# The sums of a feature DFT's result, moved from GpSimd to VectorE in single steps

## The chip, the cores and the metric

The kernel runs on one core of a Trainium2 chip. The metric is the device time of one execution in microseconds. The core has five engines that run side by side and meet through semaphores: TensorE (PE in the profile, its weight loads PEld) for matrix products, VectorE (DVE), ScalarE (ACT), GpSimd (POOL), and SyncE (SP), which here issues every DMA.

## The reference

The reference is a transformer block of two sublayers over 2048 tokens with 448 features. The first is Fourier mixing, the second a gated GELU network with 1792 hidden columns:

```python
def _A_ref(x, dft_seq_re, dft_seq_im, dft_hid_re, dft_hid_im):
    a = jnp.einsum("bsd,ed->bse", x, dft_hid_re)
    b = jnp.einsum("bsd,ed->bse", x, dft_hid_im)
    y = jnp.einsum("ts,bse->bte", dft_seq_re, a) - jnp.einsum("ts,bse->bte", dft_seq_im, b)
    return y

def _B_ref(x, w_gate, w_up, w_down):
    g = jnp.einsum("bsd,df->bsf", x, w_gate)
    u = jnp.einsum("bsd,df->bsf", x, w_up)
    h = _gelu(g) * u
    return jnp.einsum("bsf,fd->bsd", h, w_down)

h = x + _A_ref(_layernorm(x, axis=-1), A_dft_seq_re, A_dft_seq_im, A_dft_hid_re, A_dft_hid_im)
h2 = h + _B_ref(_layernorm(h, axis=-1), B_w_gate, B_w_up, B_w_down)
```

## The kernel before

All products are made from float16 operands split into a high and a low part (`hi_part` on ScalarE, `lo_part` on VectorE, lines 104 to 111), with three of the four cross terms kept.

The first half of the execution does the Fourier mixing. The tokens form 16 tiles of 128, in pairs ("units" 0 to 7). For each tile the **feature DFT** (`feature_mm`, slots "F") multiplies the normalized, transposed tile with the hidden DFT matrix into two PSUM banks `ab`, one real and one imaginary. The **sequence DFT** (`seq_mm`, slots "U") runs in 8 passes over the output tokens; in each pass every unit contributes once, with its weights `wr` loaded from HBM, split into `ws` on ScalarE and VectorE, and freed for the next load. In four of the units (`S_UNITS`: 4 to 7, tiles 8 to 15) the products go by Strassen's scheme with 7 instead of 8 block products. These need sums of the weights (`seq_sums` into `wsum`, VectorE, split into `wss`) and, once per tile, sums of the feature DFT's result: `feature_sums`. The order of units in the first pass is 0, 1, 5, 2, 6, 3, 7, 4, so that tiles 10 and 11 are the first that need `feature_sums`, then 12, 13, 14, 15, 8, 9.

For such a tile the chain is: `feature_high` (ScalarE copies the two banks to the float32 tile `b32`), `feature_sums` (three dependent operations on `b32`, lines 493 to 495, on GpSimd), `sums_high` (ScalarE, float16), `sums_low` (VectorE). For the other tiles `feature_high` (ScalarE) and `feature_low` (VectorE, line 111) read PSUM directly. Four PSUM banks serve the feature DFT, two per tile, so a tile's products can begin only when the tile before the last has been read out; the tiles come in the order ..., 10, 11, 4, 5, 12, 13, 6, 7, ....

Beside this, VectorE and ScalarE prepare the gated network's weights for 12 of 14 blocks (class `Weights`: `gu_raw` is loaded, `sums` makes `gu_s` on lines 639 to 645, four pieces are split into `gu_p` and stored to `w_dram`), and handle the finished passes (`seq_out`, moments, normalization, `ffn_sums`, splits and transposes).

The order on each engine is written by a **planner**. `add` makes a task with an engine, a cost, a due time and what it must follow; `chain` makes one task for each `yield` of a generator. `arranged` steps through time by 0.05 us; whenever an engine is free in its model, the ready task with the earliest due time begins. Due times follow `T`, the planned start of each slot of TensorE; planner time 0 is the start of slot 3, tile 3's feature DFT, at 24.05 us in the trace. The instructions are then issued in the order found, and each engine works through its queue strictly in this order. In the model a VectorE task that begins while GpSimd is busy counts 1.6 times. `feature_sums` is one GpSimd task of 3.4 us; the only other planned GpSimd task is `down_sums(0)` near the end of the DFTs. The weight blocks' due times are spread evenly from `begin0` to 10 us before the end of the DFTs; the first sums of a block may begin 10 us before its own start time.

The second half runs the gated network and the down projection; TensorE there is fed by `gw` loads from `w_dram`, and GpSimd does other sums.

Of the kernel before, what the change touches and what calls it, by code (L numbers as in the profile page):

```python
# [32 lines left out]
def kernel(  # L33
# [38 lines left out]
    V, A, G, PE = nc.vector, nc.scalar, nc.gpsimd, nc.tensor  # L72
# [257 lines left out]
    def x_load(u, parts=(slice(0, 2),)):  # L330
        if parts[0].start == 0:
            t = pair_tile(f"x{u}")
            for g in range(2):
                xt[2 * u + g] = t[:, g, :], t[:, parts[0], :]
        for s in parts:
            src = x_pairs[u][:, s, :]
            t = xt[2 * u + s.start]
            nc.sync.dma_start(t[1] if s.start == 0 else t[0], src if s.start == 0 else src[:, 0, :])
# [9 lines left out]
    def x_stats(*tiles):  # L348
        n, tag = len(tiles), f"x{tiles[0]}"
        mv = norm_x[tiles] = small.tile([P, n, 2], F32, tag=f"mv{n}", name=f"mv_{tag}")  # L350
        sts = [small.tile([P, 6], F32, tag="st", name=f"st_x{i}") for i in tiles]
        for i, st in zip(tiles, sts):
            V.bn_stats(st, xt[i][0])  # L353
        for g, st in enumerate(sts):
            V.bn_aggr(mv[:, g, :], st)

    def x_root(*tiles):
        norm_x[tiles] = norm_x[tiles], root(norm_x[tiles], f"x{tiles[0]}")

    def x_rstd_steps(*tiles):  # L360
        mv, sd = norm_x.pop(tiles)
        found = []
        steps = rstd_steps(found, mv, sd, f"x{tiles[0]}")
        next(steps)
        for g, i in enumerate(tiles):
            norm_x[i] = mv, found[0], g
        yield
        yield from steps

    def x_rstd(*tiles):  # L370
        for _ in x_rstd_steps(*tiles):
            pass

    def x_bias(*tiles):
        mv, r, _ = norm_x[tiles[0]]
        nb = small.tile([P, len(tiles)], F32, tag=f"nb{len(tiles)}", name=f"nb_x{tiles[0]}")
        bias_of(nb, mv, r)
        for i in tiles:
            norm_x[i] += (nb,)

    def x_norm(i):
        x_norm_v(i)
        x_high(i)
# [25 lines left out]
    def x_turn(i):  # L409
        xT_tile(i)  # L410
        nc.sync.dma_start_transpose(xT[i], xs[i])
# [79 lines left out]
    def feature_sums(i, E):  # L491
        b = b32[i]
        E.tensor_sub(b[:, 4:6], b[:, 0:1].to_broadcast([P, 2, HD]), b[:, 1:3])
        E.tensor_sub(b[:, 6], b[:, 2], b[:, 4])
        E.tensor_sub(b[:, 7], b[:, 3], b[:, 6])

    def sums_high(i):
        t = bop[i] = dft.tile([P, 2, 7, HD], F16, name=f"b{i}")
        hi_part(t[:, 0], b32[i][:, 1:8])
# [233 lines left out]
    FIRST = 3  # L733
    COST = {"F": 4.16, "P": 4.54, "S": 4.02}
    spans = [COST["F" if s[0] == "F" else "S" if is_s(s[2]) else "P"] for s in slots]
    T = {n: sum(spans[FIRST:n]) - sum(spans[n:FIRST]) for n in range(len(slots) + 1)}
    tasks, steps = [], {}

    def add(*args, **kw):
        tasks.append(Task(*args, **kw))  # L740
        return tasks[-1]

    def chain(engine, costs, due, make, after=()):

        run, last = [], list(after)

        def step(first):
            if first:
                run.append(make())
            next(run[0])  # L750

        for k, cost in enumerate(costs):
            last = [add(engine, cost, due, lambda k=k: step(k == 0), after=last)]
        return last[0]
# [4 lines left out]
    def fixed(n, rank, engine, cost, what, after=(), lag=0.0):  # L759
        if n < FIRST:  # L760
            plan(n, rank, what)
            return None
        return add(engine, cost, T[n + 1], what, after=after, begin=T[n] - 1.0, lag=lag)
# [3 lines left out]
    for k, (i, i2) in enumerate(tiles_of):  # L767
        n = where["F", i]
        if k > 2:
            t = fixed(n - 10, 8, "SP", 0.1, lambda u=i // 2: x_load(u), lag=5.0)  # L770
            t = fixed(n - 7, 7, "V", 1.35, lambda i=i, j=i2: x_stats(i, j), [t])
            t = fixed(n - 6, 2, "A", 0.3, lambda i=i, j=i2: x_root(i, j), [t])
            if n - 6 < FIRST:
                fixed(n - 6, 5, "V", 0.6, lambda i=i, j=i2: x_rstd(i, j))
            else:
                t = chain("V", (0.2, 0.1, 0.1, 0.1), T[n - 5], lambda i=i, j=i2: x_rstd_steps(i, j), [t])
            t = fixed(n - 6, 5, "V", 0.15, lambda i=i, j=i2: x_bias(i, j), [t])
        for c in (i, i2):
            n = where["F", c]
            if k > 2:  # L780
                low = fixed(n - 5, 5, "A", 1.15, lambda i=c: x_norm(i), [t])
                low = fixed(n - 5, 5, "V", 0.85, lambda i=c: x_lo(i), [low])
            if k >= 2:
                turned[c] = fixed(n - 4, 2, "SP", 0.1, lambda i=c: x_turn(i), [low] if k > 2 else (), lag=5.0)
                steps[n].after += [t for t in [turned[c]] if t]
        for c in (i, i2):
            n = where["F", c]
            if not k:
                continue
            done = [steps[n]] if n in steps else []  # L790
            if is_s(c // 2):
                t = drained = add("A", 1.05, T[n + 1] + 1.5, lambda i=c: feature_high(i), after=done + ring_w[-2:][:1] * (len(ring_w) > 1))
                t = add("G", 3.4, T[n + 2], lambda i=c: feature_sums(i, G), after=[t])
                t = add("A", 1.45, T[n + 2] + 2.0, lambda i=c: sums_high(i), after=[t])
                t = add("V", 1.7, T[n + 2] + 3.5, lambda i=c: sums_low(i), after=[t])
                ring_w.append(t)
            else:
                t = add("A", 0.95, T[n + 1] + 1.0, lambda i=c: feature_high(i), after=done)
                t = drained = add("V", 1.07, T[n + 1] + 2.5, lambda i=c: feature_low(i), after=[t])
            bop_of[c] = t  # L800
            out_of[n] = drained
# [11 lines left out]
    for g, (p, u) in enumerate(units):  # L813
        n = where["U", p, u]
# [14 lines left out]
        if is_s(u):  # L829
            t = chain("V", (0.6, 0.34, 0.34), T[n] - 3.0, lambda p=p, u=u: seq_sums(p, u), [load] + sums_of)  # L830
# [11 lines left out]
    for p in range(N_PASS):  # L842
        q, j = divmod(p, 2)
        of_pass = [where["U", p, u] for u in range(N_UNIT)]
        n0, n = min(of_pass), max(of_pass) + 1
# [12 lines left out]
        t = add("A", 0.25, t0 + 14.0, lambda q=q, j=j: ffn_root(q, j), after=m)  # L858
        t = chain("V", (0.2, 0.1, 0.1, 0.1), t0 + 15.0, lambda q=q, j=j: ffn_rstd_steps(q, j), [t])
        last_e, h_done[p] = m, [store, t]  # L860
        if q < 2:
            t = add("V", 0.15, t0 + 16.0, lambda q=q, j=j: ffn_bias(q, j), after=[t])
            t = add("A", 1.35, t0 + 17.0, lambda q=q, j=j: ffn_norm_act(q, j, hp[q, j]), after=[t])
            h_done[p] = [store, t]
            for k in range(4):
                t = add("V", 0.36, t0 + 18.0 + k, lambda q=q, j=j, k=k: ffn_sums(q, j, (k,)), after=[t])
            for k in range(2):
                high = add("A", (0.65, 1.0)[k], t0 + 22.0 + k, lambda q=q, j=j, k=k: ffn_hi(q, j, (k,)), after=[t])
                t = high
            for k in range(5):  # L870
                t = add("V", (0.34, 0.87, 0.25, 0.35, 0.25)[k], t0 + 23.0 + k, lambda q=q, j=j, k=k: ffn_lo(q, j, (k,)), after=[t])
# [17 lines left out]
        gu[f] = Weights(f, p2, None)  # L889

    plan(0, 9, lambda: gu_begin(order[0]))
    begin0 = 20.0
    raw, freed, stages = None, [], []
    for k, f in enumerate(order):
        gap = (at_end - 10.0 - begin0) / N_DFT
# [4 lines left out]
        t, lows = s2, []  # L900
        for m in range(4):
# [4 lines left out]
            t = high  # L906
# [7 lines left out]
    t = fixed(len(slots) - 14, 9, "SP", 0.1, lambda: down_load(0), last_e, lag=6.0)  # L914
# [2 lines left out]

    def arranged():

        now, left, busy, begun, n = 0.0, list(tasks), {"V": 5.6, "A": 4.7, "G": 0.0, "N": 0.0}, [], FIRST  # L920
        busy["SP"] = busy["PE"] = 0.0

        def ready(t):
            return t.begin <= now and all(a.end is not None and a.end + a.lag <= now for a in t.after)

        while left or n < len(slots):
            if n < len(slots) and busy["PE"] <= now and ready(steps[n]):
                steps[n].end = busy["PE"] = now + spans[n]
                begun.append((now, n))
                n += 1  # L930
            for engine in ("SP", "N", "V", "A", "G"):
                if busy[engine] > now:
                    continue
                able = [t for t in left if t.engine == engine and ready(t)]
                if able:
                    t = min(able, key=lambda t: t.due)
                    cost = t.cost * (1.6 if engine == "V" and busy["G"] > now else 1.0)
                    t.end = busy[engine] = now + cost
                    begun.append((now, t))
                    left.remove(t)  # L940
            now += 0.05
            assert now < 2 * at_end
        return begun
# [448 lines left out]
    for t in range(3 * NF, N_GU):  # L1392
        f = t % NF
        if f < NF - 1:
            n, k = divmod(f, 2)
# [196 lines left out]
```

## Time and profile before

| | us |
|---|---|
| Median of three runs | 718.97 |
| Lowest and highest | 717.75, 719.52 |
| The profiled execution | 719.33 |
| Its span, first to last instruction | 717.6 |
| TensorE busy in it | 707.3 |
| VectorE, ScalarE, GpSimd busy | 519.6, 396.4, 212.2 |

A timeline row gives the start in us, the time covered in us, engine, line, operation, what is written from what, the tile's form and a count; in square brackets stands the engine's idle time before it and what ended it. A row of waits reads: who waited for whom, us in total, times, the longest. A row of groups gives busy us and mean ns of one, then the idle time before. DVE line 111 and ACT line 105 are helpers, so such a row is told apart by its tile's name.

### The profile page before, as it was taken

Reading aid. Unit: us, or ns where it says so; the run is one execution under the profiler, and the core shown is the slowest. Engines: PE = TensorE matmul, PEld = TensorE weight load, DVE = VectorE, ACT = ScalarE, POOL = GpSimd, SP = SyncE. Lnnn points to the kernel's source line nnn. Section 1 sums busy time; section 2 is a strip of 40 time slices with the busy share of each in tenths; the row PEclk is TensorE's granted clock in tenths of the full one; section 3 lists DMA queues with packets and bytes.
Section 4 is the critical chain, followed back from the end, with each engine's and each line's share of the span. In section 5 each row is a group of like instructions: output and inputs, shape, how many; then the busy total and the mean of one; then the engine's idle time right before and its main releaser. Section 6 shows DMA issues by size and latency. Waiting matters only on the chain.

```text
span 717.6 us, 15058 instructions
## 1 busy us (share of the span) xinstructions
PE 707.3 (99%) x5944; PEld 575.6 (80%) x5944; DVE 519.6 (72%) x1054; ACT 396.4 (55%) x836; POOL 212.2 (30%) x241
## 2 busy tenths in 40 slices
PE   8998999999999999999999999999999999999998
PEld 5555567777776777686888899999999999999998
DVE  6898889999896988978368667575765756677520
ACT  5676655767474764645166575555555545555500
POOL 0033042000000000001015664375664755557230
PEclk9999999999999999999999999999999999999999
DMA  9466555887987898748258754847568686655401
GB/s 330 113 148 164 99 192 180 296 203 264 246 256 193 260 282 278 252 163 320 99 203 327 259 182 161 189 162 202 178 188 193 184 214 209 214 179 206 156 14 65
DMA packets 83815, 143.85 MB, mean 200 GB/s; under 512 B 41888, under 2 KB 60448, under 8 KB 83744
## 3 DMA queue, kind: packets, MB, share of 16 engines
q1 hardware_dynamic: 83744, 142.89, 64.8%
q8 instruction: 46, 0.75, 0.4%
q14 instruction: 25, 0.20, 0.1%
HBM read 113.38 MB, written 20.19 MB: 186 GB/s over the span
## 4 chain that ended last, share of the span: by engine, by line
PE 82%; DVE 10%; ACT 3%; DMA 2%; issue 2%; SPq 1%; DVEq 0%; ACTq 0%
PE acc L570 31%; PE pY L1173 13%; PE acc_d L1118 11%; PE pZ L1173 9%; PE pX L1173 9%; PE ab L456 5%; DMA wr<-in_w_seq_dram 1%; DVE ws L111 1%; PE last_Z L1335 1%; PE last_X L1335 1%; PE last_Y L1335 1%; DVE xs L109 1%; DMA wh_raw<-in_w_hid_dram 1%; DVE b L111 1%; DVE st_x L353 1%
## 5 line engine op out<-in xcount | busy, mean ns | idle before, releaser
L1173 PEld LDWEIGHTS <-gw 128*128 128x128 f16 x2184 | 213.4, 98 | 23.3 <-issue 1.4
L570 PE MATMUL acc<-b,ws 128*128 128x448 f16 (+1 forms) x1344 | 222.0, 312 | 0.1
L570 PEld LDWEIGHTS <-ws 128*128 128x128 f16 x1344 | 130.6, 98 | 71.1 <-DVE ws L111 0.4
L1173 PE MATMUL pY<-hops,gw 128*128 128x256 f16 x952 | 129.1, 273 | 0.0
L1118 PE MATMUL acc_d<-wd,dn_w 128*128 128x224 f16 x882 | 105.1, 259 | 0.0
L570 PE MATMUL acc<-b,wss 128*128 128x224 f16 x768 | 94.8, 259 | 0.7 <-DVE wss L111 0.7
L1118 PEld LDWEIGHTS <-dn_w 128*128 128x128 f16 x882 | 85.1, 98 | 2.8
L1173 PE MATMUL pZ<-hops,gw 128*128 128x256 f16 x616 | 85.5, 273 | 0.7 <-DVE hh L1183 0.6
L105 ACT ACTIVATE ws<-wr 128x256 f16<-128x256 f32 (+2 forms) x96 | 62.6, 690 | 40.8 <-DMA wr<-in_w_seq_dram 22.9
L1173 PE MATMUL pX<-hops,gw 128*128 128x256 f16 x616 | 83.3, 273 | 0.0
L234 POOL TENSOR_TENSOR wd_s<-wd 128x448 f32<-128x448 f32 x7 | 8.5, 1209 | 244.1 <-ACT ws L105 225.0
L111 DVE SCALAR_TENSOR_TENSOR ws<-wr,ws 128x256 f16<-128x256 f32 (+2 forms) x96 | 73.9, 797 | 6.6 <-ACT ws L105 6.5
L570 PEld LDWEIGHTS <-wss 128*128 128x128 f16 x768 | 73.9, 98 | 1.2 <-DVE wss L111 1.2
L1252 POOL TENSOR_TENSOR hh<-hh,c 128x256 f32<-128x256 f32 x42 | 32.5, 777 | 109.7 <-ACT c L1250 109.5
L456 PEld LDWEIGHTS <-xT 128*128 128x128 f16 x352 | 34.7, 99 | 35.6 <-issue 5.3
L109 DVE TENSOR_TENSOR dn_w<-hh,dn_w 128x256 f16<-128x256 f32 x42 | 19.6, 466 | 53.1 <-ACT dn_w L105 53.1
L1266 POOL TENSOR_TENSOR dn_s<-hh 128x256 f32<-128x256 f32 x42 | 52.9, 1259 | 0.0
L105 ACT ACTIVATE wss<-wsum 128x1024 f16<-128x1024 f32 x32 | 33.7, 1053 | 31.7 <-DVE wsum L518 31.7
L109 DVE TENSOR_TENSOR dn_w<-dn_s,dn_w 128x640 f16<-128x640 f32 x42 | 46.3, 1103 | 6.2 <-ACT dn_w L105 4.6
L1217 ACT ACTIVATE u<-pY 128x256 f32<-128x256 f32 x56 | 21.4, 382 | 52.1 <-PE pY L1173 52.1
L456 PE MATMUL ab<-wh_hi,xT 128*128 128x448 f16 x224 | 47.1, 361 | 2.4 <-DVE b L111 2.3
L1212 ACT ACTIVATE pY<-pX 128x256 f32<-128x256 f32 x56 | 20.6, 368 | 49.9 <-PE pX L1173 49.9
(135 smaller groups left out, 984.9 us busy)
## 6 DMA issues: line engine op xcount, KB each, us to landing
gw<-w_dram SPq DMA_DIRECT2D x54, 896.0 KB, 5.1
wr<-in_w_seq_dram SPq DMA_DIRECT2D x64, 512.0 KB, 4.9
gu_raw<-in_w_gu_dram SPq DMA_DIRECT2D x28, 384.0 KB, 4.4
w_dram<-gu_p SPq DMA_DIRECT2D x36, 256.0 KB, 2.9
wd<-in_w_down_dram SPq DMA_DIRECT2D x14, 448.0 KB, 4.7
hx<-in_x_dram SPq DMA_DIRECT2D x8, 448.0 KB, 5.9
h_dram<-hx SPq DMA_DIRECT2D x8, 448.0 KB, 4.2
hr<-h_dram SPq DMA_DIRECT2D x8, 448.0 KB, 5.4
```

The source lines that it names most:

```text
L105: A.activation(dst, src, AF.Copy, scale=scale)
L109: V.tensor_sub(dst, src, hi)
L111: V.scalar_tensor_tensor(dst, src, scale, hi, op0=ALU.mult, op1=ALU.subtract)
L456: PE.matmul(feat[i][r][:, :D], xT[i][:, kx, :], w[:, kw, r * D : (r + 1) * D], start=n == 0, stop=n == 10,)
L570: PE.matmul(banks[k][:, cols], lhs, rhs, start=k not in begun, stop=stop, skip_group_check=True)
L1118: PE.matmul(acc[k // 2][:, k % 2 * HD : (k % 2 + 1) * HD], a_of(la, a), b_of(lb, b), start=first and m == 0 and k % 2 == 0, stop=last and ...
L1173: PE.matmul(ps, w[:, wl, wa + ws, :], ops[:, m + ms, :], start=first and n == 0, stop=last and n == len(terms) - 1, skip_group_check=True,)
L1212: A.activation(self.Y, self.X, AF.Copy)
L1217: A.activation(self.u2, self.Y, AF.Copy, scale=SC)
L1252: G.tensor_mul(c22, c22, self.c12)
L1266: G.tensor_sub(s[:, 2:4], t[:, 1:4:2], t[:, 0:4:2])
L1335: PE.matmul(banks[0][:, c * HD : (c + 1) * HD] if one else banks[c][:, 0:HD], last["h"][:, lh, f, tok], w, start=f == 0 and m == 0 and c = ...
```

## The change

Three places. `feature_sums` yields after each of its operations, and the planner runs it as a chain of three VectorE tasks (0.56, 0.36 and 0.36 us) with the same due time, in place of the one GpSimd task. In `arranged` the factor 1.6 is replaced: a VectorE task that begins beside a busy GpSimd is counted at 1.9 times its cost for the part that lies beside it, and a GpSimd task that begins beside a busy VectorE lengthens that VectorE task in the same way. And `begin0`, the start of the weight blocks' spread, goes from 20 to 12.

```diff
     def feature_sums(i, E):
         b = b32[i]
         E.tensor_sub(b[:, 4:6], b[:, 0:1].to_broadcast([P, 2, HD]), b[:, 1:3])
+        yield
         E.tensor_sub(b[:, 6], b[:, 2], b[:, 4])
+        yield
         E.tensor_sub(b[:, 7], b[:, 3], b[:, 6])
+        yield
...
-                t = add("G", 3.4, T[n + 2], lambda i=c: feature_sums(i, G), after=[t])
+                t = chain("V", (0.56, 0.36, 0.36), T[n + 2], lambda i=c: feature_sums(i, V), [t])
...
-    begin0 = 20.0
+    begin0 = 12.0
...
-        now, left, busy, begun, n = 0.0, list(tasks), {"V": 5.6, "A": 4.7, "G": 0.0, "N": 0.0}, [], FIRST
+        now, v, left, busy, begun, n = 0.0, None, list(tasks), {"V": 5.6, "A": 4.7, "G": 0.0, "N": 0.0}, [], FIRST
...
-                    cost = t.cost * (1.6 if engine == "V" and busy["G"] > now else 1.0)
+                    cost = t.cost
+                    if engine == "V":
+                        beside = min(max(busy["G"] - now, 0.0), 1.9 * cost)
+                        cost += beside * 0.9 / 1.9
+                        v = t
+                    elif engine == "G" and busy["V"] > now:
+                        v.end = busy["V"] = busy["V"] + 0.9 * min(busy["V"] - now, cost / 1.9)
```

## The prediction

> **What bounds the kernel now.** I read the page first: TensorE is busy for almost the whole span, so only its idle time and its slow time can be won. Then the waits with TensorE's rows alone, which say where that idle time is.
>
> ```profile
> PE 707.3 (99%) x5944; PEld 575.6 (80%) x5944; DVE 519.6 (72%) x1054; ACT 396.4 (55%) x836; POOL 212.2 (30%) x241
> ...
> PE ab L456 <- DVE b L111: 2.3, 2, 2.1
> PE pw L99 <- POOL eps_t L91: 1.4, 1, 1.4
> PE xT_ps L418 <- ACT xs L105: 1.0, 1, 1.0
> PE acc L570 <- DVE wss L111: 0.7, 1, 0.7
> ```
>
> The first and fourth lie in the stage that the change touches: 2.3 us behind VectorE's `b` (line 111) and 0.7 us behind its `wss`. The other two are the start. The timeline of TensorE and the windows around the first wait:
>
> ```profile
> 52.43 1.68 PE L456 MATMUL ab<-wh_lo,xT 128*128 128x448 f16 x8
> 56.19 0.35 PE L456 MATMUL ab<-wh_hi,xT 128*128 128x448 f16 x1 [2.09 <-DVE b L111]
> 56.72 4.28 PE L456 MATMUL ab<-wh_hi,xT 128*128 128x448 f16 x13 [0.18 <-DVE b L111]
> ...
> 62.37 2.81 PE L456 MATMUL ab<-wh_hi,xT 128*128 128x448 f16 x14
> ...
> 57.40:60.80 3.40, 3.40 (x12) 1.33 (x10) 3.40 (x11) 0.40 (x2) 0.00 (x0) 0.52 0.58 109
> ...
> 227.40:230.80 3.40, 2.60 (x19) 1.40 (x17) 3.40 (x7) 2.73 (x7) 0.00 (x0) 1.00 0.48 154
> ```
>
> In the windows the columns are the stretch, its length, the busy time of PE, PEld, DVE, ACT and POOL, the granted clock, DMA share and GB/s. TensorE stands still for 2.09 + 0.18 = 2.27 us before the feature DFT of tile 12 (its PSUM banks are those of tile 4, freed by `feature_low(4)`), and the 3.4 us after that run at clock 0.52: 3.4 x (1 - 0.52) = 1.63 us more. The stall costs 3.9 us in all. The stall near 230 us was shorter and left the clock at 1.00.
>
> In a sentence of its own: the Trainium skill, "TensorE: Matmul & The Clock Gate", What's actually happening, puts the fall to half rate behind an idle window of about 3.4 us; this trace shows the fall after 2.27 us, so by that rule the sum below would lose its clock term, and by the trace it keeps it.
>
> **Why VectorE is late there.** The timelines of VectorE and GpSimd up to the stall, and the unstretched form of the same operations:
>
> ```profile
> 40.21 1.36 DVE L640 TENSOR_TENSOR gu_s<-gu_raw 128x256 f32<-128x256 f32 x1
> 41.49 0.61 DVE L147 SCALAR_TENSOR_TENSOR r_x<-r_x 128x2 f32<-128x2 f32 x1
> 42.61 0.77 DVE L645 TENSOR_TENSOR gu_s<-gu_raw,gu_s 128x256 f32<-128x256 f32 x1
> ...
> 47.16 1.09 DVE L147 SCALAR_TENSOR_TENSOR r_x<-r_x 128x2 f32<-128x2 f32 x1
> 48.51 0.61 DVE L157 SCALAR_TENSOR_TENSOR nb_x<-mv_x,r_x 128x2 f32<-128x2 f32 x1
> 49.04 1.48 DVE L111 SCALAR_TENSOR_TENSOR ws<-wr,ws 128x256 f16<-128x256 f32 x2
> 53.21 1.79 DVE L109 TENSOR_TENSOR b<-b,b 128x1568 f16<-128x1568 f32 x1 [0.98 <-ACT b L105]
> 55.52 1.15 DVE L111 SCALAR_TENSOR_TENSOR b<-ab,b 128x448 f16<-128x448 f32 x2
> ...
> 75.51 0.42 DVE L640 TENSOR_TENSOR gu_s<-gu_raw 128x256 f32<-128x256 f32 x1
> 77.64 0.42 DVE L645 TENSOR_TENSOR gu_s<-gu_raw,gu_s 128x256 f32<-128x256 f32 x1
> 129.17 1.02 DVE L111 SCALAR_TENSOR_TENSOR ws<-wr,ws 128x256 f16<-128x256 f32 x2
> 138.58 0.15 DVE L147 SCALAR_TENSOR_TENSOR r_h<-r_h 128x2 f32<-128x2 f32 x1
> 139.25 0.15 DVE L157 SCALAR_TENSOR_TENSOR nb_h<-mv_h,r_h 128x2 f32<-128x2 f32 x1
> ```
>
> ```profile
> 39.94 1.34 POOL L493 TENSOR_TENSOR b<-b 128x448 f32<-128x448 f32 x1 [37.69 <-DVE r_x L145]
> 42.16 0.93 POOL L495 TENSOR_TENSOR b<-b 128x224 f32<-128x224 f32 x1
> 47.05 1.18 POOL L493 TENSOR_TENSOR b<-b 128x448 f32<-128x448 f32 x1 [3.96 <-ACT b L105]
> 49.18 0.79 POOL L495 TENSOR_TENSOR b<-b 128x224 f32<-128x224 f32 x1
> ```
>
> Each stretched VectorE operation ends as a GpSimd sum ends or runs beside it. Even an operation on 2 columns goes from 0.15 to 1.09 us: it waits for the whole instruction of the other engine. The stretch beside the sums of tiles 10 and 11 is (1.36-0.42) + (0.61-0.15) + (0.77-0.42) + (1.09-0.15) + (0.61-0.15) + (1.48-1.02) = 3.61 us.
>
> **The change part by part.**
>
> *Sums off GpSimd.* For these two tiles 3.61 us of stretch leave VectorE.
>
> *Sums onto VectorE.* Per tile one 128x448 and two 128x224 float32 operations. No VectorE row has exactly these; the nearest are these groups:
>
> ```profile
> L617 DVE TENSOR_TENSOR hx<-hx,e 128x448 f32<-128x448 f32 x4 | 2.5, 615 | 0.0
> ...
> L518 DVE TENSOR_TENSOR wsum<-wsum,wr 128x256 f32<-128x256 f32 x32 | 13.4, 418 | 0.2
> ```
>
> Upper bound 0.615 + 2 x 0.418 = 1.45 us; lower bound, since neighbours overlap (the pair at 55.52 takes 1.15 us for two such rows of 0.61), 0.54 + 2 x 0.31 = 1.16 us. I take 1.3: the steps depend on one another, but other work is put between. Two tiles cost 2.6 us, so VectorE's own load before the stall falls by 3.61 - 2.6 = 1.0 us.
>
> *What the shorter operations release.* The stall is reached through ScalarE too, so its timeline counts:
>
> ```profile
> 43.48 0.76 ACT L389 ACTIVATE x<-x,nb_x,r_x 128x448 f32<-128x448 f32 x1 [2.85 <-DVE nb_x L157]
> ...
> 49.15 0.76 ACT L389 ACTIVATE x<-x,nb_x,r_x 128x448 f32<-128x448 f32 x1 [0.78 <-DVE nb_x L157]
> ...
> 51.68 1.49 ACT L105 ACTIVATE b<-b 128x1568 f16<-128x1568 f32 x1
> 54.34 0.96 ACT L105 ACTIVATE b<-ab 128x448 f16<-128x448 f32 x2
> ```
>
> ScalarE waits for the small `r_x`, `nb_x` steps, which are most urgent by due time and are held up only by whatever runs before each. Ahead of 43.48 the stretch is 0.94 + 0.46 + 0.35 = 1.75 us; sums of tile 10 would displace other work there, not add to it, since only one operation fits between two of these steps. Ahead of 49.15 it is 1.75 + 0.94 + 0.46 = 3.15 us, less 1.3 for the sums of tile 10 (due first): 1.85, or 0.55 if those of tile 11 also come before. I take the smaller of the two upper values. ScalarE, which has no other idle time up to 54.34, then runs 1.75 us earlier; `feature_high(4)` begins near 52.6 and `feature_low(4)` near 53.8 instead of 55.5. TensorE is free at 52.43 + 1.68 = 54.1, so about 2.27 - 1.75 = 0.5 us of stall is left. That is below the 0.8 us (3.40 - 2.60) that left the clock alone near 230 us, so the 1.63 us go as well. Bounds of the released time: 0.55 us (1.7 us of stall left) and the full 2.27 us.
>
> *GpSimd's latency.* From 39.94 to 43.09 the sums took 3.15 us; three VectorE steps take 1.3. Nothing waits for the difference here: ScalarE reaches the split later in both. Cost nothing, gain nothing.
>
> *The steps' yields, and the queue behind them.* On GpSimd a wait for ScalarE's `b` cost nobody anything; on VectorE everything queued behind waits. That is the price in the slow rival. In the sum it is nothing, because VectorE is behind ScalarE up to 57 us.
>
> *The planner.* With the sums gone GpSimd holds one planned task (`down_sums(0)`, in the trace from 336.5 us, where TensorE has no wait), so the 1.9 rule acts on almost nothing. `begin0` 20 to 12 brings the first weight block's due times 8 us forward, the last one's 8/12 = 0.7. The first sums (39.74 us in the trace) still lose to every more urgent task of VectorE, which was busy without a break there: I put its move at nothing, between +0.4 us (one more 128x256 low part, the 0.42 class, ahead of `feature_low(4)`) and -0.9 (half of the first block's sums drawn into earlier gaps). SP's queue gets the stores and loads of these blocks with them, in changed places.
>
> *The other six tiles and the give-back.* Each adds 1.3 us and takes away between nothing and 1.8 (half of 3.61). VectorE's cover, from the windows:
>
> ```profile
> 60.80:104.00 43.20, 43.20 (x271) 26.30 (x270) 36.03 (x58) 25.57 (x41) 15.42 (x15) 1.00 0.68 173
> 104.00:183.00 79.00, 79.00 (x614) 58.95 (x613) 75.21 (x146) 51.54 (x92) 4.45 (x3) 1.00 0.74 227
> 183.00:230.60 47.60, 46.80 (x348) 33.10 (x345) 37.61 (x81) 27.29 (x53) 0.00 (x0) 1.00 0.89 233
> ...
> 185.63 0.39 DVE L608 SCALAR_TENSOR_TENSOR e<-acc,e 128x224 f32<-128x224 f32 x1 [2.36 <-PE acc L570]
> ...
> 225.02 0.69 DVE L514 TENSOR_TENSOR wsum<-wr 128x512 f32<-128x512 f32 x1 [4.74 <-DMA wr<-in_w_seq_dram]
> ```
>
> VectorE is idle for 7.2 us in the first, 3.8 in the second, 10.0 in the third. If TensorE comes 3.4 us earlier, it meets `wss` at 230 us 3.4 us earlier; VectorE follows by 2.36 us at once, as it stood waiting for TensorE at 185.63, and needs 1.0 us more out of 11 us of earlier idle time. I take 0.3 us of give-back, between 0 and, if the load that lands at 225 us does not move, all 3.4.
>
> **Sum.** 719.33 (the profiled execution; span 717.6) - 1.75 (stall) - 1.63 (clock) + 0.3 = 716.25. The median 718.97 is 0.36 below that execution: 715.9. The likeliest one's own range is 714.6 to 717.5.
>
> **Rivals.**
>
> *Half a stall stays* (13%): ScalarE's order, not the stretch, holds `feature_high(4)`, and only 1.0 us is won, with the clock still falling: 718.0. For it: ScalarE runs without a gap from 49.15 to the stall. Against: that run starts at a wait for VectorE.
>
> *The gain comes back at 230 us* (13%): the `wr` load that lands at 225 us is late because SP issued it behind transposes and a store; then TensorE's lead of 3.4 us becomes a longer wait for `wss`: 718.6 to 719. Against it: 2.36 us of VectorE's wait follow TensorE. The Trainium skill, "Perfetto Trace Analysis", Optimizing Scalar/DVE Operations, warns that moving work between these two engines might not help since they share a port; by that, this case or the next; the 3.61 us of stretch against 2.6 us of new work speak against it.
>
> *The change does nothing it should* (3%): the planner's order absorbs it: 719.
>
> *Head-of-line waits, slower* (18%): the sums stand in VectorE's strict order before `feature_low` or a weight's low part, and wait for ScalarE. It decides as soon as VectorE reaches a sum before ScalarE's `feature_high` has ended, by more than the 1.0 us that its load falls. GpSimd's row at 47.05 waited 3.96 us for `b`; the whole of it on VectorE, less 1.0, makes the stall 3.0 us longer and draws another window to half clock (1.63): 723.6; half of it makes 1.0 us, or 2.6 with the window: 720 to 721.6. I take 722. For it: that row. Against: VectorE was late there, not early.
>
> **How the numbers follow.** Forecast 53%. A measurement of this kernel tells about 0.3% (2.2 us) from no change: faster is below 716.8, slower above 721.1. Most of the forecast (48 of 53) is faster, as is some of the first two rivals (4); slower is most of the last rival (15) and 2 for stalls not thought of. So 0.52, 0.31, 0.17. The range 713.9 to 721.8 leaves a tenth at the lower end (both stalls gone and earlier weights helping) and a tenth above.
>
> **What would show it.** Right: no POOL rows before 336 us; line 147 and 157 rows of 0.15 us throughout; the wait of `ab` behind `b` below 0.8 us and no stretch below clock 0.9 after 20 us; the `wss` wait near 230 us (then 227) at most 1 us. Wrong: VectorE idle before lines 493 to 495 with `ab` waiting longer; or `ab`'s wait gone and as much new waiting for `ws` or `wss`.

## The result and the profile after

The changed kernel takes 714.08 us (median of four, 713.76 to 714.77); the kernel before, beside it, 718.36 (717.42 to 719.52). The ratio is 0.9941, with a 95% interval of 0.9926 to 0.9957: 4.3 us faster, where 3.1 were forecast. The profiled execution of the changed kernel took 713.92 us with a span of 712.1, against 719.33 and 717.6.

From the page of the changed kernel the engines' busy times, and from its waits two of TensorE's rows and the first of GpSimd's:

```profile
PE 704.3 (99%) x5944; PEld 574.7 (81%) x5944; DVE 517.5 (73%) x1078; ACT 396.8 (56%) x836; POOL 187.2 (26%) x217
...
PE xT_ps L418 <- ACT xs L105: 1.6, 2, 1.0
...
PE pZ L1182 <- DVE hh L1192: 0.3, 1, 0.3
...
POOL wd_s L234 <- DMA wr<-in_w_seq_dram: 330.9, 1, 330.9
```

Neither `ab` behind `b` nor `acc` behind `wss` is left; what remains belongs to the start and to the second half. VectorE is not busier than before (517.5 against 519.6 us), although it now has the sums. GpSimd does nothing between its start and `down_sums(0)`.

The timeline of TensorE around tile 12, and windows in the columns explained above, changed kernel:

```profile
52.77 1.68 PE L456 MATMUL ab<-wh_lo,xT 128*128 128x448 f16 x8
54.28 2.81 PE L456 MATMUL ab<-wh_hi,xT 128*128 128x448 f16 x14
...
58.45 2.81 PE L456 MATMUL ab<-wh_hi,xT 128*128 128x448 f16 x14
```

```profile
54.00:57.40 3.40, 3.40 (x20) 1.76 (x19) 3.38 (x10) 3.26 (x7) 0.00 (x0) 1.00 1.09 340
57.40:60.80 3.40, 3.40 (x20) 1.76 (x19) 3.40 (x10) 0.98 (x2) 0.00 (x0) 1.00 0.60 142
...
183.00:230.60 47.60, 47.60 (x357) 34.36 (x356) 41.09 (x85) 30.78 (x61) 0.00 (x0) 1.00 0.86 253
```

Tile 12 follows tile 5 without a gap, at full clock, and there is no idle time of TensorE near 230 us. Tile 12 takes 58.45 - 54.28 = 4.17 us to the start of tile 13; before it took 62.37 - 53.94 = 8.43 (53.94 being where 52.43 plus eight products of the pace above ends). That is 4.26 of the 5.5 us between the two spans. The rest is the stall near 230 us, some 0.8 us, and smaller differences between the two places and behind them, less a start that happened to be 0.34 us later.

The timelines of VectorE and ScalarE up to there, changed kernel:

```profile
40.97 0.62 DVE L493 TENSOR_TENSOR b<-b 128x448 f32<-128x448 f32 x1
41.50 0.15 DVE L157 SCALAR_TENSOR_TENSOR nb_x<-mv_x,r_x 128x2 f32<-128x2 f32 x1
41.62 0.39 DVE L495 TENSOR_TENSOR b<-b 128x224 f32<-128x224 f32 x1
...
43.70 0.39 DVE L497 TENSOR_TENSOR b<-b 128x224 f32<-128x224 f32 x1
...
53.10 1.15 DVE L111 SCALAR_TENSOR_TENSOR b<-ab,b 128x448 f16<-128x448 f32 x2
```

```profile
41.69 0.76 ACT L389 ACTIVATE x<-x,nb_x,r_x 128x448 f32<-128x448 f32 x1 [1.54 <-DVE nb_x L157]
...
49.24 1.51 ACT L105 ACTIVATE b<-b 128x1568 f16<-128x1568 f32 x1 [0.82 <-DVE r_x L143]
50.74 0.76 ACT L389 ACTIVATE x<-x,nb_x,r_x 128x448 f32<-128x448 f32 x1
...
52.01 0.96 ACT L105 ACTIVATE b<-ab 128x448 f16<-128x448 f32 x2
52.86 0.76 ACT L389 ACTIVATE x<-x,nb_x,r_x 128x448 f32<-128x448 f32 x1
...
54.13 1.04 ACT L105 ACTIVATE wss<-wsum 128x1024 f16<-128x1024 f32 x1
```

The sums take 0.62 + 0.39 + 0.39 = 1.40 us, in single steps among other work, and the small operations are short. `feature_low(4)` begins at 53.10 in place of 55.52. But ScalarE's rows show something the forecast had not reckoned with: not only is each operation earlier, they stand **in another order**. Before, the split of tile 11's sums (51.68) and `feature_high(4)` (54.34) came behind the x step of tile 6, a `gu_p` piece and the first `wss` split, with the x step of tile 7 between them. These are the rows of the kernel before that the prediction does not show, the `gu_p` piece, the `wss` split and tile 7's x step:

```profile
50.43 0.40 ACT L105 ACTIVATE gu_p<-gu_raw 128x256 f16<-128x256 f32 x1
50.73 1.04 ACT L105 ACTIVATE wss<-wsum 128x1024 f16<-128x1024 f32 x1
...
53.08 0.74 ACT L389 ACTIVATE x<-x,nb_x,r_x 128x448 f32<-128x448 f32 x1
```

Now the split of tile 11's sums comes first, and tile 7's x step and the `wss` split stand behind `feature_high(4)`. Two theories are thus open: **stretch** (VectorE was slowed by GpSimd, the forecast's reason) and **order** (the planner writes better queues when the sums are VectorE tasks).

### The profile page after: what moved, and what is told of

Read it like the earlier page. It is cut to its first block, busy times and chain, and to the rows that moved or that the text cites. A ratio compares the mean times of both kernels' runs of the same rounds, so it can differ in the third digit from the quotient of the medians.

```text
span 712.1 us, 15056 instructions
## 1 busy us (share of the span) xinstructions
PE 704.3 (99%) x5944; PEld 574.7 (81%) x5944; DVE 517.5 (73%) x1078; ACT 396.8 (56%) x836; POOL 187.2 (26%) x217
## 4 chain that ended last, share of the span: by engine, by line
PE 94%; DVE 2%; ACT 1%; DMA 1%; issue 1%; SPq 0%; DVEq 0%; ACTq 0%
PE acc L573 38%; PE pY L1182 14%; PE acc_d L1127 11%; PE pZ L1182 9%; PE pX L1182 9%; PE ab L456 9%; PE last_Z L1344 1%; PE last_X L1344 1%; PE last_Y L1344 1%; DMA wh_raw<-in_w_hid_dram 1%; PE last_a L1344 1%; PE last_tr L1344 1%; DVE dn_w L109 0%; ACT dn_w L105 0%; DVE wh_lo L111 0%
## 5 line engine op out<-in xcount | busy, mean ns | idle before, releaser
L111 DVE SCALAR_TENSOR_TENSOR ws<-wr,ws 128x256 f16<-128x256 f32 (+2 forms) x96 | 71.9, 778 | 9.8 <-ACT ws L105 9.6
L111 DVE SCALAR_TENSOR_TENSOR wss<-wsum,wss 128x1024 f16<-128x1024 f32 x32 | 39.9, 1247 | 9.7 <-ACT wss L105 9.6
L456 PE MATMUL ab<-wh_hi,xT 128*128 128x448 f16 x224 | 45.6, 352 | 0.3 <-ACT wh_hi L105 0.2
```

The lines of the kernel that those rows point to most:

```text
L111: V.scalar_tensor_tensor(dst, src, scale, hi, op0=ALU.mult, op1=ALU.subtract)
L456: PE.matmul(feat[i][r][:, :D], xT[i][:, kx, :], w[:, kw, r * D : (r + 1) * D], start=n == 0, stop=n == 10,)
```

## The experiments

### Engine and order apart

The first kernel keeps the old plan, and so every queue's order, and only issues the sums on VectorE:

```diff
-                t = add("G", 3.4, T[n + 2], lambda i=c: feature_sums(i, G), after=[t])
+                t = add("G", 3.4, T[n + 2], lambda i=c: feature_sums(i, V), after=[t])
```

> Edit: the kernel before, whose planner still plans the sums as one GpSimd task of 3.4 us, so every queue keeps its order; only the engine that is issued changes, to VectorE, at the place in the order where the GpSimd task stood. Theory (the stall at tile 12 came from the stretch of VectorE's operations beside GpSimd's, 3.6 us against 2.6 us of sums): most of the gain comes without any new order; the wait of ab behind b falls from 2.3 us to at most 1.2 us, no half clock at 57 us, time 2.5 to 4 us below the kernel before. Rival (the new order of the queues is what helps, the engine is not): within 1 us of the kernel before, or slower, the wait stays near 2.3 us.

Measured: 718.02 us against 718.79, ratio 0.9992 (0.9974 to 1.0009): no change. TensorE's wait, and VectorE's and ScalarE's timelines of this kernel:

```profile
PE ab L456 <- DVE b L111: 1.9, 2, 1.7
...
41.11 0.62 DVE L493 TENSOR_TENSOR b<-b 128x448 f32<-128x448 f32 x1
41.76 0.39 DVE L494 TENSOR_TENSOR b<-b 128x224 f32<-128x224 f32 x1
42.19 0.39 DVE L495 TENSOR_TENSOR b<-b 128x224 f32<-128x224 f32 x1
42.50 0.15 DVE L147 SCALAR_TENSOR_TENSOR r_x<-r_x 128x2 f32<-128x2 f32 x1
...
51.87 1.49 ACT L105 ACTIVATE b<-b 128x1568 f16<-128x1568 f32 x1
```

Every stretched row is gone (line 147 takes 0.15 us), and it buys 0.4 us of the stall. In the old order the three sums stand together ahead of the urgent step on line 147, 42.50 - 41.11 = 1.39 us, and take the place of the stretch. The theory of the stretch fails for the most part.

The second kernel is the reverse: the changed kernel's plan, with the operations issued on GpSimd.

```diff
-                t = chain("V", (0.56, 0.36, 0.36), T[n + 2], lambda i=c: feature_sums(i, V), [t])
+                t = chain("V", (0.56, 0.36, 0.36), T[n + 2], lambda i=c: feature_sums(i, G), [t])
```

> Edit: the changed kernel, whose planner plans three VectorE steps with the new costs and due times, but the three operations are issued on GpSimd. Same order as the changed kernel. Theory (stretch): the small r_x and nb_x operations on lines 147 and 157 take 0.6 to 1.1 us again, ab waits 1.5 to 3 us before tile 12, time within 1.5 us of the kernel before or above it. Rival (order): 3 to 4.5 us below the kernel before, as the changed kernel.

Measured: 715.15 us, ratio 0.9949 (0.9929 to 0.9968). The wait, rows of VectorE and ScalarE, and the window behind the stall in this kernel:

```profile
PE ab L456 <- DVE b L111: 0.9, 2, 0.7
...
40.44 1.36 DVE L643 TENSOR_TENSOR gu_s<-gu_raw 128x256 f32<-128x256 f32 x1
41.72 0.61 DVE L147 SCALAR_TENSOR_TENSOR r_x<-r_x 128x2 f32<-128x2 f32 x1
...
50.51 1.51 ACT L105 ACTIVATE b<-b 128x1568 f16<-128x1568 f32 x1 [1.23 <-POOL b L497]
...
57.40:60.80 3.40, 3.40 (x20) 1.76 (x18) 3.40 (x10) 2.18 (x5) 0.20 (x1) 1.00 0.92 200
```

The stretch is back, 1.36 and 0.61 us as in the kernel before, and still the stall is only 0.9 us and the clock stays full. **Order** carries most of the gain. With the changed kernel's 714.08 the four corners are: old order 718.4 to 718.8 on GpSimd and 718.0 on VectorE; new order 715.2 on GpSimd and 714.1 on VectorE. The engine's own share in the new order, some 1 us, has its row in the 0.9 us of stall, but the intervals of the two ratios overlap. ScalarE's row shows a second cause for it beside the stretch: the split of tile 11's sums now waits 1.23 us for GpSimd's last sum. No run tells how much of the 0.9 us is the stretch and how much this wait.

### The parts of the change

The sums as planned VectorE steps, without the new cost rule and with `begin0` at 20, as a diff against the changed kernel:

```diff
-    begin0 = 12.0
+    begin0 = 20.0
...
-                    cost = t.cost
-                    if engine == "V":
-                        beside = min(max(busy["G"] - now, 0.0), 1.9 * cost)
...
+                    cost = t.cost * (1.6 if engine == "V" and busy["G"] > now else 1.0)
```

> Edit: the kernel before with the sums as three planned VectorE steps, and neither the new cost rule nor the new begin0. Theory (now: the gain is in the order that the planner writes once the sums are VectorE tasks): within 0.7 us of the changed kernel, 714 to 715. Rival (the two planner edits are needed with it): 716 or above, with a wait of ab, ws or wss behind VectorE.

Measured: 714.30 us, ratio 0.9937 (0.9922 to 0.9952). This part alone is the whole gain. The next takes only `begin0` back:

```diff
-    begin0 = 12.0
+    begin0 = 20.0
```

> Edit: the changed kernel with begin0 at 20 again; sums on VectorE in single steps and the new cost rule stay. Theory (begin0 was put at nothing, between 0.4 us worse and 0.9 us better, at the stall): within 1 us of the changed kernel, the wait before tile 12 below 0.8 us. Rival (the earlier weight blocks carry a part of the gain, at tile 12 or near 230 us): 1 to 3 us above the changed kernel, with a wait of ab, ws or wss to show for it.

Measured: 714.11 us, ratio 0.9931 (0.9906 to 0.9957): `begin0` does nothing in the changed kernel, as forecast. Nor does the split into steps, taken back here:

```diff
-                t = chain("V", (0.56, 0.36, 0.36), T[n + 2], lambda i=c: feature_sums(i, V), [t])
+                t = add("V", 1.28, T[n + 2], lambda i=c: list(feature_sums(i, V)), after=[t])
```

> Edit: the changed kernel, with the three sums of a tile planned as one VectorE task of 1.28 us in place of three steps. Theory: the steps matter little, since what counts is that GpSimd is out of the way: within 0.7 us of the changed kernel. Rival (the steps let the urgent r_x and nb_x operations in between, so they carry the gain on ScalarE's side): ScalarE's wait for nb_x at 41 us grows by about 0.7 us, and the time by 1 us or more with a stall before tile 12.

Measured: 714.41 us, ratio 0.9936 (0.9916 to 0.9956); 0.2 us of stall before tile 12. The planner finds another good order for one longer task. Then the other two parts in the kernel before, each alone:

```diff
-    begin0 = 20.0
+    begin0 = 12.0
```

> Edit: the kernel before with begin0 at 12; sums on GpSimd, old cost rule. Theory (nothing by itself): within 1 us of the kernel before, with the wait of ab before tile 12 between 1.8 and 2.7 us. Rival (the weight blocks' place is what cleared the stall): 2 to 4 us below the kernel before.

Measured: 718.43 us, ratio 0.9997 (0.9983 to 1.0012): nothing. And the cost rule as in the change's diff, with the sums left on GpSimd:

> Edit: the kernel before with the new cost rule alone (1.9 times for the part that lies beside, both ways); sums on GpSimd, begin0 at 20. With the sums on GpSimd the rule acts on eight tasks, so the order does change. Theory (the stretch stays, whatever the order): within 1.5 us of the kernel before, the stretched rows are still there. Rival (a true cost lets the planner order round the stretch): 2 to 4 us below the kernel before.

Measured: 723.89 us, ratio 1.0072 (1.0046 to 1.0097): 5 us slower. Neither theory expected this. Its waits of TensorE:

```profile
PE acc L570 <- DVE wss L111: 2.1, 3, 0.9
PE acc L570 <- DVE ws L111: 1.7, 1, 1.7
...
PE acc L570 <- ACT wss L105: 1.3, 1, 1.3
...
PE ab L456 <- DVE b L111: 0.2, 1, 0.2
```

The stall before tile 12 is down to 0.2 us, by order alone, with every sum still on GpSimd. But the new order opens others, at 116, 183 and 232 us, and behind the first and the last of them the clock falls as well: in windows of 3.4 us from 115.4 on it is 0.80 and 0.70, from 232.4 on 0.66 and 0.84, some 1.7 us each. A truer cost rule did not make a better plan.

Last, the planner is told that the GpSimd task takes as long as the VectorE steps:

```diff
-                t = add("G", 3.4, T[n + 2], lambda i=c: feature_sums(i, G), after=[t])
+                t = add("G", 1.28, T[n + 2], lambda i=c: feature_sums(i, G), after=[t])
```

> Edit: the kernel before, whose planner counts the GpSimd task of the sums at 1.28 us in place of 3.4; engine, old rule and begin0 as before. On ScalarE the split of tile 11's sums and feature_high(4) now come ahead of the first wss split, and feature_high(4) ahead of both x steps of tiles 6 and 7. Theory (order): the wait of ab before tile 12 is below 1.2 us. The time is 2 us or more below the kernel before if nothing else in the new order stalls, but GpSimd's sums really take 3 us, so waits for POOL can open elsewhere. Rival (stretch): ab waits 1.8 us or more, time as before.

Measured: 718.80 us, ratio 0.9997 (0.9983 to 1.0011), a miss for the theory of the order in its simple form. The wait of `ab`, and ScalarE's timeline in this kernel:

```profile
PE ab L456 <- DVE b L111: 2.6, 2, 2.4
...
43.87 1.51 ACT L105 ACTIVATE b<-b 128x1568 f16<-128x1568 f32 x1 [3.32 <-POOL b L495]
...
52.01 1.51 ACT L105 ACTIVATE b<-b 128x1568 f16<-128x1568 f32 x1 [1.72 <-POOL b L495]
53.74 0.96 ACT L105 ACTIVATE b<-ab 128x448 f16<-128x448 f32 x2
```

ScalarE has `feature_high(4)` ahead of the `wss` split, but it now stands 3.32 and 1.72 us waiting for sums that the plan thought done, with everything behind them queued. An order written for short sums needs them to be short.

### ScalarE's order by itself

In the kernel before, three ScalarE tasks are moved by hand from before `feature_high(4)` to right behind it; nothing else is touched. They carry a mark `move`, that task the mark `anchor`:

```diff
-    for _, t in arranged():
+    planned = [t for _, t in arranged()]
+    late_a = [t for t in planned if isinstance(t, Task) and t.move]
+    planned = [t for t in planned if t not in late_a]
+    here = next(k for k, t in enumerate(planned) if isinstance(t, Task) and t.anchor) + 1
+    planned[here:here] = late_a
+    for t in planned:
```

> Edit: the kernel before with its planned order, engines and costs, and one thing moved by hand: on ScalarE the x step of tile 7 (1.26 us), the wss split of unit 5 (0.95 us) and a gu_p piece (0.3 us), which stood before feature_high(4), are issued right behind it; the split of tile 11's sums moves up by the last two. All else keeps its order. Theory (ScalarE's strict order is what made feature_high(4) late): sums_low of tile 11 begins 1.3 us earlier, ab waits 0.8 to 1.2 us in place of 2.3, no half clock, time 1 to 3 us below the kernel before. Rival (VectorE's load, not ScalarE's order): ab waits 1.8 us or more, time within 0.7 us of the kernel before.

Measured: 716.83 us, ratio 0.9971 (0.9947 to 0.9994). The wait, and the timelines of ScalarE and VectorE:

```profile
PE ab L456 <- DVE b L111: 1.2, 2, 1.0
...
51.00 1.49 ACT L105 ACTIVATE b<-b 128x1568 f16<-128x1568 f32 x1
52.40 0.96 ACT L105 ACTIVATE b<-ab 128x448 f16<-128x448 f32 x2
...
51.01 3.48 DVE L109 TENSOR_TENSOR b<-b,b 128x1568 f16<-128x1568 f32 x2
55.02 1.14 DVE L111 SCALAR_TENSOR_TENSOR b<-ab,b 128x448 f16<-128x448 f32 x2
```

In the traced execution three moved tasks halve the stall. The interval of the ratio nearly reaches 1, so the rows carry this reading more than the time does; TensorE's waits also list 1.1 us for `acc` behind `wss`, against 0.7 in the kernel before. The two `sums_low` now follow each other without the 0.98 us of idle time between them; what is left of the stall lies on VectorE, which is busy throughout.

The reverse, in the changed kernel: the x step of tile 7 and the `wss` split are put back in front of `feature_high(4)` (the same code without `+ 1`, and with two marks).

> Edit: the changed kernel with its order, and on ScalarE two tasks put back in front of feature_high(4) as they stood in the kernel before: the x step of tile 7 and the wss split of unit 5, 2.1 us together. The sums stay on VectorE. Theory (ScalarE's order): feature_high(4) begins near 54.1 in place of 52.0, ab waits 1 to 1.5 us again, time 1 to 1.5 us above the changed kernel, and up to 3 if the clock falls too. Rival (with GpSimd out of the way there is room): no wait above 0.3 us, within 0.4 us of the changed kernel.

Measured: 715.70 us, ratio 0.9957 (0.9942 to 0.9972), so 1.6 us above the changed kernel; the intervals of the two ratios overlap, but each of its four executions is slower than each of the changed kernel's four. The wait, ScalarE and VectorE in this kernel:

```profile
PE ab L456 <- DVE b L111: 1.2, 2, 1.0
...
53.19 1.04 ACT L105 ACTIVATE wss<-wsum 128x1024 f16<-128x1024 f32 x1
54.13 1.83 ACT L105 ACTIVATE b<-ab 128x448 f16<-128x448 f32 x4
...
54.69 1.16 DVE L111 SCALAR_TENSOR_TENSOR b<-ab,b 128x448 f16<-128x448 f32 x2 [1.59 <-ACT b L105]
```

With the sums on VectorE and no GpSimd work nearby, two tasks in front of `feature_high(4)` leave VectorE idle for 1.59 us and bring 1.2 us of stall back.

### The price of the stall

In the changed kernel, `sums_low` of tile 11 is issued twice, or three times, so that VectorE reaches `feature_low(4)` 1.79 or 3.58 us later:

```diff
+        for _ in range(2 if i == 11 else 1):   # the second kernel: 3
             lo_part(bop[i][:, 1], b32[i][:, 1:8], bop[i][:, 0])
```

> Edit: the changed kernel with sums_low of tile 11 issued twice (the same values written again): 1.79 us more of VectorE right ahead of feature_low of tile 4, the last thing before the place of the old stall. Measures the price of the stall by itself. In the changed kernel the second bank is read out as tile 12 could begin, so a stall of about 1.7 us comes back. Theory (stall and clock both cost): 1.7 us, and 1.6 us more if the next 3.4 us fall to half clock: 1.7 to 3.4 us above the changed kernel. Rival (the loss is made up later, since the second stage of waits near 230 us has room): within 0.7 us.

> Edit: the changed kernel with sums_low of tile 11 issued three times: 3.58 us more of VectorE ahead of feature_low of tile 4. Theory: a stall of about 3.4 us, the next window at half clock (1.6 us): 5.0 us above the changed kernel, clock column near 0.5 for 3.4 us. Rival (no clock price): 3.4 us above. Rival (made up later): below 2 us.

Measured: 715.62 us for the first (ratio 0.9973, 0.9960 to 0.9986) and 718.68 for the second (1.0000, 0.9983 to 1.0017): 1.5 and 4.6 us above the changed kernel. The wait and the window behind it, the first kernel and then the second:

```profile
PE ab L456 <- DVE b L111: 1.3, 2, 1.1
...
57.40:60.80 3.40, 3.40 (x19) 1.76 (x18) 3.40 (x11) 1.74 (x4) 0.00 (x0) 1.00 0.36 68
```

```profile
PE ab L456 <- DVE b L111: 3.1, 2, 3.0
...
57.40:60.80 3.40, 3.06 (x10) 1.29 (x10) 3.40 (x11) 0.82 (x2) 0.00 (x0) 0.67 0.65 121
60.80:64.20 3.40, 3.40 (x17) 1.61 (x15) 3.40 (x9) 0.45 (x2) 0.00 (x0) 0.83 0.22 62
```

The delays came out as stalls of 1.3 and 3.1 us, where about 1.7 and 3.4 were expected. A stall of 1.3 us costs about its own length; one of 3.1 us costs 1.5 us more, the 3.4 x (0.33 + 0.17) = 1.7 us that the lower clock takes. The executions of the second kernel show the two prices apart: three of ten had a mean clock of 1.00 and took 717.29 to 717.63 us, 3.2 to 3.6 above the changed kernel, and the seven at 0.997 or 0.998 took 718.55 to 719.35. Nothing is made up later. The longer delay puts the time back where the kernel before had it, though with a longer stall (3.1 us for 2.3) and none near 230 us.

## Why the prediction was right or wrong, point by point

**What bounds the kernel**: right. Most of the gain lies where the prediction looked, at tile 12 and near 230 us, and a stall made by hand costs about its own length, and 1.5 us more where the clock falls.

**The stretch**: its size was read rightly (3.6 us), its worth was not. With the queues unchanged, the sums on VectorE fill the place of the stretch, and the stall falls by 0.4 us.

**The sums on VectorE**: taken at 1.3 us per tile, measured 1.40.

**What the shorter operations release** is the step that failed. It said that the sums "would displace other work there, not add to it, since only one operation fits between two of these steps". In the old order all three fit, and did. It gave ScalarE 1.75 us by the stretch alone; the split of tile 11's sums came 51.68 - 49.24 = 2.4 us earlier, mostly since other ScalarE work was queued behind it. The prediction treated the plan as fixed (**the planner** was weighed only for its cost rule and `begin0`), though moving a task from one engine to another in a plan rewrites every queue. The chance given to "the planner's order absorbs it" had the right object and the wrong sign.

**GpSimd's latency**: put at nothing, since ScalarE reached the split later anyway. That holds for the old order only; in the new order with the sums on GpSimd, ScalarE waits 1.23 us for them.

**The clock term** was right in size, 1.63 us, but it is not paid in every execution; see below.

**The give-back**: put at 0.3 us, it was a gain of some 0.8: the stall near 230 us vanished. Why it vanished stays open. TensorE's waits list no `acc` in the kernel with the new order on GpSimd, but they list none either with the engine alone moved or with `begin0` alone changed, so it does not take the changed kernel's order to lose this stall.

**`begin0`**: put at nothing, measured at nothing. **The rule**: put at nothing with the sums gone, measured at nothing there; that it makes the kernel slower without the move was not foreseen.

**Rivals.** *Half a stall stays* had the right reason at 13%: it said that ScalarE's order, not the stretch, holds `feature_high(4)`, and the three moved tasks bear that out. It took that order as fixed, and its outcome came only where it was: the engine moved alone kept 1.9 us of stall. The gain lost at 230 us and head-of-line waits did not come about: VectorE stood idle for 0.6 us in all before line 493. The warning from the Trainium skill, "Perfetto Trace Analysis", Optimizing Scalar/DVE Operations, that moving work between GpSimd and VectorE might not help, agrees with the engine moved alone (ratio 0.9992), but not with the move planned as VectorE steps (0.9937).

**The sum**: 3.1 us forecast, 4.3 measured. That is inside the range (713.9 to 721.8), close to its lower end, and below the likeliest case's own range (714.6 to 717.5); the stall term was 1.75 and measured 2.27, and the give-back had the wrong sign. That the number came out near is luck in part: the stall was taken as mostly gone for a reason that, with the queues unchanged, carries 0.4 of its 2.3 us.

What stays open: which quantity of the plan (the longer GpSimd task, or the 1.6 on VectorE beside it) wrote the poor order. Shortening the task alone gave another order, with other waits, and so did the other cost rule.

## What to carry to other kernels

Where a planner or a list of due times writes the queues, moving an operation is two changes: its engine and everybody's order. Test them apart, by planning it on one engine and issuing it on the other. And read the stall's chain through every strict queue: here the engine named by the wait, VectorE, was itself behind three ScalarE tasks that were not urgent.

## What the runs showed of the hardware that was not expected

The same stall does not always lower the clock. In the kernel with `begin0` alone changed, the profiled execution has a longer wait than the kernel before and full clock behind it:

```profile
PE ab L456 <- DVE b L111: 2.6, 2, 2.4
...
57.40:60.80 3.40, 3.40 (x20) 1.76 (x19) 3.40 (x11) 0.29 (x1) 0.00 (x0) 1.00 0.89 197
```

That execution took 716.58 us, at a mean clock of 0.999; one other of this kernel took 716.66 at 1.00, and the remaining eight 717.8 to 719.7, all at 0.997. The kernel before is divided in the same way: of its 54 executions beside the experiments, 24 had a mean clock of 0.999 or 1.00 (median 717.3 us) and 30 a lower one (median 719.1 us). So the clock term is in only about half of the executions behind its median.

The engine moved alone had a shorter stall, 1.9 us, and fell to clock 0.53 in the same window:

```profile
57.40:60.80 3.40, 3.40 (x11) 1.43 (x10) 3.40 (x12) 0.59 (x2) 0.00 (x0) 0.53 0.65 121
```

And the kernel planned short, whose row of waits is the same as the one above (2.6, 2, 2.4), fell to 0.73 and 0.77 in the two windows from 57.40 on. So behind a stall of about 1.9 to 3.1 us the fall comes or not: the kernel with 3.1 us kept its clock in three executions of ten. Before tile 12 no trace shows it behind 1.3 us or less. Five of the 40 executions of the kernels whose traces show at most 1.3 us there (leaving out the cost rule alone, which stalls elsewhere) had a mean clock of 0.997 or 0.998 as well, but these were not traced, so where their clock fell is not known.

The Trainium skill, "TensorE: Matmul & The Clock Gate", What's actually happening, has the activity window run freely and not start anew with the kernel; that would make the fall a matter of phase. The runs agree with that, though none of them sets the phase. They do not bear out the idle window of about 3.4 us as a length that a single wait must have, since the fall came behind waits of 1.9 and 2.3 us.
